# Attention and MLP kernel on one core: batch 0 in a listed order of steps, means from the division's sums, first q load and sum casts on ScalarE

## Chip, cores, metric

The kernel runs on one core of one Trainium2 chip. The metric is the device time of one launch in microseconds; lower is better. Most executions of one kernel lie within 1% of each other here, so a difference of a few tenths of a per cent needs several runs in the same rounds.

## The reference

Eight batches, eight heads, 576 tokens, head size 64. Causal attention with a bias from a running sum of `s`, then, token by token, an MLP whose output is added to its input:

```python
scores = scale * q @ k.T                       # per batch and head
cum    = cumsum(max(s, 0))
scores = where(causal, -1e9, scores + min(-(cum_i - cum_j), 0))
attn   = softmax(scores) @ v                   # [8, 8, 576, 64]
x      = attn.transpose(0, 2, 1, 3).reshape(8, 576, 512)
mu, var = mean(x), mean((x - mu)**2)           # per token
xn     = (x - mu) / sqrt(var + 1e-6) * g_ln
out    = x + max(xn @ w_ch1, 0) @ w_ch2        # 512 -> 2048 -> 512
```

## The kernel before

From batch 1 on, heads are interleaved with the MLP of the batch before, and TensorE is full. Batch 0 has no MLP before it to interleave with, so it runs in its own way, by token tiles: the rows of q, k and bias of 128 tokens are transposed, their scores, exponentials, value products, division and mean follow, and quarter "pieces" of the MLP's first product fill in. This stage (here "the front") ends where the heads of batch 1 begin. A "pair" is the q and k of two heads, w1 and w2 are the weights of the two products, loaded in four parts each, and rstd is the reciprocal deviation of the normalisation. The parts that matter below:

```python
def tile_pv(t, g):                     # value products, division, statistics of one tile
    ...
    nc.vector.reciprocal(out=rinv[:, 0:G], in_=pot[:, :, D])
    nc.vector.tensor_tensor(out=x..., in0=pot[:, :, 0:D], in1=rinv..., op=ALU.mult)
    nc.vector.bn_stats(out=st[0][:, t, g, :], in_=x)

def aug(gam, eng, h0=0):               # bias rows of a head group, four small copies in SBUF
    eng.dma_start(out=kq[i][D : D + 1, 1, h0:G, 0:S], in_=c_hi[r, :])
    for j in range(3):
        eng.dma_start(out=kq[i][D + 1 + j : D + 2 + j, 0, h0:G, 0:S], in_=c3[r, j, :])
...                                    # cut: the front's steps, in order
last_keys()                            # last scores of batch 0: the old bias rows are free
aug(2, nc.sync)                        # bias rows for the first heads of batch 1
piece(0, 3, "act")
tr_pair(4)                             # q and k of those heads, transposed
evac_pair("k", 4, ("dve", "dve"))
evac_pair("q", 4, ("act", "act"))
piece(1, 3, "dve")
last_pv(0)
last_pv(1)
bias_rows(trc)

for n in range(H, BH):                 # heads of batch 1 and later
    pre(n)                             # n == 8: loads of pairs 6, 7, w2(0), w2(1)
    ...                                # n == 10: loads of w2(2), w2(3), pair 8 (GpSimd's queue)
    scores(b, h)
    run_units(1, True)                 # hidden pieces of batch 0, then its output products
```

The softmax here doesn't subtract the row's maximum and nothing guards it: scores larger than these inputs give would overflow.

Of the kernel before, what the change touches and what calls it, by code (L numbers as in the profile page):

```python
# [15 lines left out]
P = 128  # L16
# [3 lines left out]
def kernel(  # L20
# [57 lines left out]
    mhalf = const.tile([P, 8], F32, name="mhalf")  # L78
    v_bf = [const.tile([P, NT, H, D + 1], BF16, name=f"v_bf{i}") for i in range(2)]
# [46 lines left out]
    def ld_tile(kind, t):  # L126
        tmp = stage.tile([P, H, D], F32, name="tiletmp", tag="st")
        nc.sync.dma_start(out=tmp, in_=tile_src(kind, t))
        loaded[kind, t] = tmp
# [123 lines left out]
    def cum_relu(c0, c1):  # L253
        nc.vector.tensor_scalar(
            out=c_in[:, c0:c1],
            in0=c_in[:, c0:c1],
            scalar1=0.0,
            scalar2=1.0 / scale,
            op0=ALU.max,
            op1=ALU.mult,  # L260
        )

    def cum_split(c0, c1):
        x, y, hi, mid, lo = (a[:, c0:c1] for a in (c_sc, c_in, c_hi, c_mid, c_lo))
        nc.vector.tensor_copy(out=hi, in_=x)
        nc.vector.tensor_tensor(out=y, in0=x, in1=hi, op=ALU.subtract)
        nc.vector.tensor_copy(out=mid, in_=y)
        nc.vector.tensor_tensor(out=lo, in0=y, in1=mid, op=ALU.subtract)
# [209 lines left out]
    def ln_xn(b, t):  # L478
        tiles = x_tiles(b)
        if t >= len(tiles):  # L480
            return
        ln_aggr(b, t)
        xn = xnp.tile([P, Dm], BF16, name="xn", tag="xn")
        nc.vector.scalar_tensor_tensor(  # L484
            out=xn,
            in0=tiles[t],
            scalar=mvs[b][:, t, 0:1],
            in1=gb,
            op0=ALU.subtract,
            op1=ALU.mult,  # L490
        )
        xns[b, t] = xn
        if t == len(tiles) - 1:
            ln_rstd(b)

    def ln_tr(b, t, eng="dve"):
# [3 lines left out]
        pool, tag = (ps_m, "m") if b == 0 else (ps_t, "tr")  # L500
        tr = pool.tile([P, KD, P], BF16, name="trx", tag=tag)
        for kd in range(KD):
            nc.tensor.transpose(tr[:, kd, :], xn[:, kd * P : (kd + 1) * P], ident)  # L503
        if t < NF:
# [91 lines left out]
    ld_tile("k", 0)  # L596
    ld_tile("q", 0)
# [40 lines left out]
    nc.gpsimd.memset(er[TL:P, :, OD : OD + TL], 0.0)  # L638
    nc.gpsimd.memset(er[:, :, OD + TL : EW], 0.0)
# [4 lines left out]
    ld_w1(3)  # L644

# [4 lines left out]
    trt = {}  # L650

    def tr_tile(t):
        pn = P if t < NF else TL
        for g in range(2):
            tr = ps_m.tile([P, 2, G, P], BF16, name="trt", tag="m")
            for u in range(2):
                for hh in range(G):
                    nc.tensor.transpose(  # L658
                        tr[0:KA, u, hh, 0:pn],
                        rowb[0:pn, t, u * H + g * G + hh, :],  # L660
                        ident[0:pn, 0:pn],
                    )
            trt[t, g] = tr

    def evac_tile(t, g, eng):
# [4 lines left out]
            trt.pop((t, g))[0:KA, :, :, 0:pn],  # L670
# [4 lines left out]
    def tile_bank(t, g, i):  # L675
        a = ps_s.tile([P, 512], F32, name="st", tag="s")
        for c in range(4):
            hh, kb = divmod(4 * i + c, t + 1)
            nc.tensor.matmul(
                a[:, c * P : (c + 1) * P],  # L680
                lhsT=kq[g][0:KA, 0, hh, kb * P : (kb + 1) * P],
                rhs=kq[g][0:KA, 1, hh, t * P : (t + 1) * P],
# [7 lines left out]
        o = (0, 2, 6, 0)[t] + g * (t + 1) + i  # L690
        nc.scalar.activation(out=er_slot(o), in_=a, func=ACT.Exp, scale=scale)
# [5 lines left out]

    def tile_pv(t, g):
        pot = ps_t.tile([P, G, D + 1], F32, name="pot0", tag="tr")
        for hh in range(G):  # L700
            for kb in range(t + 1):
                i, c = divmod(hh * (t + 1) + kb, 4)
                o = (0, 2, 6, 0)[t] + g * (t + 1) + i
                nc.tensor.matmul(
                    pot[:, hh, :],
                    lhsT=er_slot(o)[:, c * P : (c + 1) * P],
# [4 lines left out]
        rinv = small.tile([P, NT], F32, name="rinv", tag="rinv")  # L711
        nc.vector.reciprocal(out=rinv[:, 0:G], in_=pot[:, :, D])
        x = xb[0][:, t, g * 256 : (g + 1) * 256]
        nc.vector.tensor_tensor(
            out=x.rearrange("p (h d) -> p h d", d=D),
            in0=pot[:, :, 0:D],
            in1=rinv[:, 0:G].unsqueeze(2).to_broadcast([P, G, D]),
            op=ALU.mult,
        )
        nc.vector.bn_stats(out=st[0][:, t, g, :], in_=x)  # L720


    def last_bank(g, i):
        a = ps_s.tile([P, 512], F32, name="st", tag="s")
        for hh in range(G):
            for w in range(2):
                kb, c = 2 * i + w, (2 * hh + w) * TL
                nc.tensor.matmul(
                    a[:, c : c + TL],
                    lhsT=kq[g][0:KA, 0, hh, kb * P : (kb + 1) * P],  # L730
                    rhs=kq[g][0:KA, 1, hh, NF * P : S],
                    start=True,
                    stop=True,
                )
        nc.scalar.activation(out=er_slot(8 + 2 * g + i), in_=a, func=ACT.Exp, scale=scale)

    def last_keys():
        a = ps_s.tile([P, 512], F32, name="st", tag="s")
        for h in range(H):
            c = slice(h * TL, (h + 1) * TL)  # L740
            nc.tensor.matmul(
                a[0:TL, c],
                lhsT=kq[h // G][0:KA, 0, h % G, NF * P : S],
                rhs=kq[h // G][0:KA, 1, h % G, NF * P : S],
                start=True,
                stop=False,
            )
            nc.tensor.matmul(
                a[0:TL, c], lhsT=ident[:, 0:TL], rhs=maskT[:, 0:TL], start=False, stop=True
            )  # L750
        nc.scalar.activation(out=er_slot(0)[0:TL], in_=a[0:TL], func=ACT.Exp, scale=scale)

    def last_pv(g):
        pot = ps_t.tile([P, G, D + 1], F32, name="pot0", tag="tr")
        for hh in range(G):
            for kb in range(NT):
                h = g * G + hh
                if kb < NF:
                    c = (2 * hh + kb % 2) * TL
                    e = er_slot(8 + 2 * g + kb // 2)[:, c : c + TL]  # L760
                    vv = v_bf[0][:, kb, h, :]
                else:
                    e = er_slot(0)[0:TL, h * TL : (h + 1) * TL]
                    vv = v_bf[0][0:TL, kb, h, :]
                nc.tensor.matmul(
                    pot[0:TL, hh, :], lhsT=e, rhs=vv, start=(kb == 0), stop=(kb == NF)
                )
        rinv = small.tile([P, NT], F32, name="rinv", tag="rinv")
        nc.vector.reciprocal(out=rinv[0:TL, 0:G], in_=pot[0:TL, :, D])
        nc.vector.tensor_tensor(  # L770
            out=xm[0][0:TL, g * 256 : (g + 1) * 256].rearrange("p (h d) -> p h d", d=D),
            in0=pot[0:TL, :, 0:D],
            in1=rinv[0:TL, 0:G].unsqueeze(2).to_broadcast([TL, G, D]),
            op=ALU.mult,
        )


    def piece(c, t, eng):
        ph = ps_m.tile([P, 4, P], F32, name="ph", tag="m")
        cols = slice(t * P, (t + 1) * P)  # L780
        for j in range(4):
            fb = 4 * c + j
            for kd in range(KD):
                nc.tensor.matmul(  # L784
                    ph[:, j, :],
                    lhsT=w1_bf[:, kd, fb * P : (fb + 1) * P],
                    rhs=xTs[0][:, kd, cols],
                    start=(kd == 0),
                    stop=(kd == KD - 1),
                )  # L790
        dst = hT[:, 4 * c : 4 * c + 4, cols]
# [5 lines left out]
    def banks(t, g, *ii):  # L797
        for i in ii:
            tile_bank(t, g, i)

    R = (P, 2 * P, S)
    cum_relu(0, R[0])
    cum_scan(0, R[0])
    cum_split(0, R[0])
    cast_tile("k", 0, "act")
    cast_tile("q", 0, "act")
    cum_relu(R[0], S)
    bias_tr(0)
    bias_cols(0, 1)
    cum_scan(R[0], R[1])  # L810
    cum_split(R[0], R[1])
    keep_warm(1)
    tr_tile(0)
    evac_tile(0, 0, "act")
    bias_tr(1)
    evac_tile(0, 1, "dve")
    bias_cols(1, 2)
    cum_scan(R[1], S)
    keep_warm(2)
    banks(0, 0, 0)  # L820
    banks(0, 1, 0)
    tr_tile(1)
    evac_tile(1, 0, "act")
    evac_tile(1, 1, "dve")
    cum_split(R[1], S)
    tile_pv(0, 0)
    tile_pv(0, 1)
    banks(1, 0, 0, 1)
    for t in (2, 3, 4):
        bias_tr(t)  # L830
    bias_cols(2, NF)
    bias_cols(NF, NT, TL)
    banks(1, 1, 0, 1)
    tr_tile(2)
    evac_tile(2, 0, "act")
    evac_tile(2, 1, "dve")
    keep_warm(2)
    banks(2, 0, 0, 1, 2)
    tile_pv(1, 0)
    tile_pv(1, 1)  # L840
    ln_xn(0, 0)
    tr_tile(3)
    evac_tile(3, 0, "dve")
    evac_tile(3, 1, "dve")
    banks(2, 1, 0, 1, 2)
    ln_xn(0, 1)
    keep_warm(2)
# [169 lines left out]
```

## Time and profile before

| | before |
|---|---|
| time, first three runs | 378.47 us median (378.07 to 379.31) |
| profiled span | 376.9 us |
| TensorE busy, whole span | 96% |
| last matmul of batch 0's scores starts | 39.38 us |
| first scores of batch 1 start | 47.78 us |
| full TensorE clock again, for good | 53.58 us |

"L526" and the like are lines of the kernel's file; line numbers differ between versions, so read the operation and the tiles. "PE" is TensorE, "DVE" VectorE, "ACT" ScalarE, "POOL" GpSimd, "SPq" SyncE's issue of a DMA. The prediction shows the busy times by stretch, TensorE's waits and the chain of waits. Two more views of this kernel are needed later. GpSimd's timeline (start, length, what, and in brackets the idle time before it and what ended it):

```profile
35.78 1.05 POOL L473 TENSOR_TENSOR rstd<-rstd,mhalf 128x4 f32<-128x4 f32 x1 [8.00 <-DVE rstd L472]
...
40.13 2.29 POOL L212 DMA_DIRECT2D w_bf<-in_moe_w_ch_dram  x3
```

GpSimd stood 8.0 us for the input of batch 0's reciprocal deviations (rstd); the loads that stand behind it in the program were issued only then, the last three parts of w2 from 40.13 on (the last two at 40.9 and 41.6). VectorE's timeline, the first step on `s`:

```profile
3.67 0.22 DVE L254 TENSOR_SCALAR c_in<-c_in 64x128 f32<-64x128 f32 x1 [1.03 <-DMA c_in<-in_s_dram]
```

### The profile page before, as it was taken

What the parts mean: (1) busy time and instruction counts of PE and PEld (TensorE: products, weight loads), DVE (VectorE), ACT (ScalarE), POOL (GpSimd) and SP (SyncE); (2) the same over time, 40 slices, a digit from 0 to 9 for tenths busy, and PEclk for the clock granted to TensorE, in tenths of its full rate; (3) what the DMA queues carried; (4) which work ended last, traced back from release to release, by engine and by line L of the source; (5) the groups of instructions that cost most, each with busy time, mean ns of one, the idle gap of its engine ahead of it and who ended that gap; (6) DMA issues with size and microseconds to landing.
All of it is one profiled execution on the core that took longest, in us unless ns stands there. A gap on an engine that the chain in (4) does not pass through costs nothing.

```text
span 376.9 us, 8560 instructions
## 1 busy us (share of the span) xinstructions
PE 359.9 (96%) x3189; PEld 204.8 (54%) x3189; DVE 202.7 (54%) x532; ACT 187.0 (50%) x357; POOL 167.4 (44%) x447
## 2 busy tenths in 40 slices
PE   7888799998999999999999999999999999999995
PEld 2677645555555555555555555555555554444444
DVE  7676546879436753684357545844485573212211
ACT  3565459777773377327732773277327613411410
POOL 9872605758756457436466556365732201000000
PEclk9899969999999999999999999999999999999999
DMA  9999994599979699839897888598920011002013
GB/s 141 169 192 110 138 198 78 140 170 215 214 169 205 163 216 211 151 97 233 172 187 197 199 175 204 124 224 190 203 71 28 2 57 57 0 31 82 1 30 84
DMA packets 164266, 52.09 MB, mean 138 GB/s; under 512 B 152848, under 2 KB 159552, under 8 KB 164224
## 3 DMA queue, kind: packets, MB, share of 16 engines
q1 hardware_dynamic: 140432, 42.95, 51.3%
q0 software_dynamic: 23392, 8.06, 20.0%
q8 instruction: 25, 0.41, 0.5%
q10 hardware_dynamic: 400, 0.52, 0.4%
q14 instruction: 17, 0.14, 0.1%
HBM read 37.11 MB, written 9.44 MB: 124 GB/s over the span
## 4 chain that ended last, share of the span: by engine, by line
PE 82%; DVE 10%; DMA 3%; ACT 2%; issue 1%; SPq 1%; ACTq 0%; DVEq 0%
PE ph L516 31%; PE py L534 29%; PE pot L423 6%; DVE xn L484 3%; PE sc L347 3%; PE sa L347 3%; PE sb L347 3%; PE trx L503 2%; DMA kq<-c 1%; PE ph L784 1%; DMA tiletmp<-in_q_dram 1%; DVE stats L457 1%; PE trt L658 1%; DVE yo L543 1%; DVE kq L98 1%
## 5 line engine op out<-in xcount | busy, mean ns | idle before, releaser
L534 PE MATMUL py<-w_bf,hT 128*128 128x512 bf16 (+1 forms) x592 | 136.5, 373 | 0.5 <-DVE yo L543 0.5
L516 PE MATMUL ph<-xT,w_bf 128*128 128x512 bf16 x480 | 115.6, 383 | 0.0
L526 ACT ACTIVATE hT<-ph 128x512 bf16<-128x512 f32 x100 | 59.7, 597 | 65.2 <-PE ph L516 63.8
L534 PEld LDWEIGHTS <-hT 128*128 128x128 bf16 x592 | 53.5, 98 | 49.0 <-issue 1.0
L516 PEld LDWEIGHTS <-w_bf 128*128 128x128 bf16 x544 | 48.9, 98 | 51.0 <-issue 4.3
L366 POOL TENSOR_SCALAR_AFFINE_SELECT er<-er 128x128 bf16<-128x128 bf16 x216 | 59.2, 298 | 34.2 <-ACT er L358 34.0
L358 ACT ACTIVATE er<-sa 128x512 bf16<-128x512 f32 x56 | 33.4, 596 | 72.3 <-PE sa L347 43.1
L187 POOL CAST rows<-rowtmp 128x512 bf16<-128x512 f32 (+1 forms) x55 | 33.9, 617 | 53.2 <-DMA rowtmp<-in_q_dram 49.1
L524 DVE TENSOR_SCALAR hT<-ph 128x512 bf16<-128x512 f32 x36 | 24.9, 692 | 60.6 <-PE ph L516 59.8
L347 PEld LDWEIGHTS <-kq 68*128 68x128 bf16 x412 | 29.9, 98 | 24.3 <-issue 3.6
L423 PEld LDWEIGHTS <-er 128*128 128x128 bf16 x840 | 33.0, 98 | 13.3 <-issue 0.3
L543 DVE SCALAR_TENSOR_TENSOR yo<-py,rstd,xb 128x512 f32<-128x512 f32 x32 | 23.9, 748 | 25.9 <-PE py L534 21.2
L431 DVE RECIPROCAL rinv<-pot 128x5 f32<-128x5 f32 x56 | 10.8, 193 | 48.1 <-PE pot L423 47.9
L423 PE MATMUL pot<-v_bf,er 128*128 128x65 bf16 x840 | 34.7, 193 | 0.0
L358 ACT ACTIVATE er<-sc 128x512 bf16<-128x512 f32 x56 | 34.3, 613 | 0.0
L358 ACT ACTIVATE er<-sb 128x512 bf16<-128x512 f32 x56 | 33.6, 600 | 0.0
L473 POOL TENSOR_TENSOR rstd<-rstd,mhalf 128x4 f32<-128x4 f32 (+1 forms) x8 | 8.8, 1094 | 38.8 <-DVE rstd L472 38.8
L100 POOL CAST v_bf<-vtmp 128x512 bf16<-128x512 f32 (+1 forms) x30 | 18.8, 627 | 15.6 <-DMA vtmp<-in_v_dram 14.3
L484 DVE SCALAR_TENSOR_TENSOR xn<-xb,mv,gb 128x512 bf16<-128x512 f32 x32 | 24.3, 761 | 1.1
L433 DVE TENSOR_TENSOR xb<-pot,rinv 128x256 f32<-128x256 f32 x56 | 23.8, 424 | 1.9
L347 PE MATMUL sa<-kq 68*128 68x512 bf16 x56 | 21.6, 385 | 1.8 <-DMA kq<-c 1.8
L347 PE MATMUL sc<-kq 68*128 68x256 bf16 (+1 forms) x200 | 22.0, 227 | 0.2
(112 smaller groups left out, 372.2 us busy)
## 6 DMA issues: line engine op xcount, KB each, us to landing
out_dram<-yo SPq DMA_DIRECT2D x32, 256.0 KB
vtmp<-in_v_dram SPq DMA_DIRECT2D x24, 256.0 KB
rowtmp<-in_k_dram SPq DMA_DIRECT2D x44, 128.0 KB
rowtmp<-in_q_dram SPq DMA_DIRECT2D x44, 128.0 KB
w_bf<-in_moe_w_ch_dram POOLq DMA_DIRECT2D x8, 512.0 KB, 9.9
v_bf<-in_v_dram POOLq DMA_DIRECT2D x8, 128.0 KB, 7.9
kq<-rows SPq DMA_TRANSPOSE x55
kp<-in_k_dram POOLq DMA_DIRECT2D x6, 144.0 KB, 8.1
```

Of the source, the lines that this page charges most:

```text
L187: nc.gpsimd.tensor_copy(out=r[0:pn, :, :, 0:D], in_=loaded.pop(("rows", gam, t))[0:pn])
L347: nc.tensor.matmul(a[:, c + a0 - q0 : c + a1 - q0], lhsT=k_cols(b, h, kb), rhs=cols, start=True, stop=not (pe_mask and diag),)
L358: nc.scalar.activation(out=e[:, o : o + 512], in_=a, func=ACT.Exp, scale=scale)
L366: nc.gpsimd.affine_select(out=e[:, o : o + P], in_=e[:, o : o + P], compare_op=ALU.is_ge, fill=0.0, base=0, pattern=[[1, P]], channel_mult ...
L423: nc.tensor.matmul(pot[:, t, :], lhsT=e[:, o : o + P], rhs=vv[:, kb, h, :], start=(kb == 0), stop=(kb == last),)
L433: nc.vector.tensor_tensor(out=xb[b][:, :, hs], in0=pot[:, 0:NF, 0:D], in1=rinv[:, 0:NF].unsqueeze(2).to_broadcast([P, NF, D]), op=ALU.mult,)
L484: nc.vector.scalar_tensor_tensor(out=xn, in0=tiles[t], scalar=mvs[b][:, t, 0:1], in1=gb, op0=ALU.subtract, op1=ALU.mult,)
L516: nc.tensor.matmul(ph, lhsT=w1_bf[:, kd, fb * P : (fb + 1) * P], rhs=xT[:, kd, :], start=(kd == 0), stop=(kd == KD - 1),)
L524: nc.vector.tensor_scalar_max(out=hT[:, fb, :], in0=ph, scalar1=0.0)
L526: nc.scalar.activation(out=hT[:, fb, :], in_=ph, func=ACT.Relu)
L534: nc.tensor.matmul(py[0], lhsT=hT[:, fb, t * P : (t + 1) * P], rhs=w2_bf[:, fb, c0:c1], start=(fb == 0), stop=(fb == FB - 1),)
L543: nc.vector.scalar_tensor_tensor(out=yo, in0=py[0], scalar=rs, in1=x[:, c0:c1], op0=ALU.mult, op1=ALU.add)
```

## The change

The intent is a front with less idle time. All steps of batch 0 are cut small and put in one list, so that no engine waits for another's whole tile. VectorE, the fullest engine there, is relieved: the mean comes from the sum that the division gives along with its output, the statistics for the variance come later, and relu and casts of the running sum go to ScalarE. The first q load is issued from ScalarE. Loads of pairs 6, 7, w2(0) and w2(1) are queued earlier. The diff, cut to its core (lines left out are marked with dots):

```diff
-    ld_tile("k", 0)
-    ld_tile("q", 0)
+    ld_tile("k", 0, nc.sync)
+    ld_tile("q", 0, nc.scalar)
...
     ld_w1(3)
+    ld_cast_pair(6)
+    ld_w2(0)
+    ld_cast_pair(7)
+    ld_w2(1)
...                                   # in the division
-        nc.vector.tensor_tensor(..., op=ALU.mult)
-        nc.vector.bn_stats(out=st[0][:, t, g, :], in_=x)
+        nc.vector.scalar_tensor_tensor(
+            scalar=1.0, op0=ALU.mult, op1=ALU.mult, accum_out=sum0[:, t, g : g + 1], **args)
+    def tile_stats(t, g):
+        nc.vector.bn_stats(out=st[0][:, t, g, :], in_=xb[0][:, t, g * 256 : (g + 1) * 256])
...                                   # in the normalisation of batch 0
-        ln_aggr(b, t)
+        nc.vector.tensor_scalar(out=mean0[:, t : t + 1], in0=sum0[:, t, 0:1],
+            scalar1=sum0[:, t, 1:2], scalar2=1.0 / Dm, op0=ALU.add, op1=ALU.mult)
...                                   # the list; T transposes, e evacuation, S scores, x exp,
+    PLAN = """                       # V values, N division, B statistics, L mean and xn,
+        ...                           # X, y xT, M piece, r relu, P, pk, pq next pair, W zeros
+        M101 M102 x410 N30 M103 S411 Sk aug r10:A L3 P x411 B21 xk M020 M120 pk pq M121 M021
+        M022 M023 M122 M123 r02:D r12:A X3 S8 B11 y3:A M010 B00 M011 M130 B30 M012 M013 B10
+        M131 M132 r01:A M133 r13:A M110 M111 M112 M113 M030 M031 r11:A M032 M033 V40 r03:A
+        V41 N40 N41
+    """
...                                   # heads of batch 1: n == 8 has its scores in the list (S8)
-        if n == 8:
-            ld_cast_pair(6); ld_w2(0); ld_cast_pair(7); ld_w2(1)
-        scores(b, h)
+        if n > H:
+            scores(b, h)
...
+        if n == H + 1:
+            bias_rows(trc)
+            for t in range(NF):
+                ln_aggr(0, t)
+            ln_rstd(0)
```

`Sk` are the last scores of batch 0, `aug` the bias copies for the next heads, `S8` the first scores of batch 1.

## The prediction

> **What bounds the kernel now.** I read the page's head first, then the busy times by stretch, then TensorE's waits, then the chain of waits over the first 60 us, and last the timelines of TensorE, VectorE and ScalarE. The busy times by stretch (length, then busy us of PE, PEld, DVE, ACT and POOL, granted clock, DMA share, GB/s):
>
> ```profile
> 0.00:16.00 16.00, 11.55 (x107) 6.81 (x107) 11.93 (x42) 7.87 (x12) 14.28 (x24) 1.00 1.61 149
> 16.00:20.00 4.00, 3.97 (x38) 3.42 (x38) 0.90 (x4) 1.64 (x3) 3.04 (x8) 0.57 1.63 185
> 20.00:42.00 22.00, 18.74 (x368) 17.50 (x366) 15.48 (x37) 13.91 (x27) 12.60 (x17) 1.00 1.34 142
> 42.00:47.80 5.80, 3.16 (x41) 2.47 (x42) 3.59 (x8) 0.79 (x1) 1.69 (x3) 0.91 1.15 163
> 47.80:53.60 5.80, 5.80 (x28) 2.93 (x29) 1.41 (x4) 2.24 (x5) 0.00 (x0) 0.50 1.22 201
> ...
> 100.00:150.00 50.00, 50.00 (x439) 27.56 (x438) 26.91 (x77) 29.06 (x58) 27.54 (x85) 1.00 0.90 192
> ```
>
> From 100 us TensorE is full, and nothing there is edited. So the change is worth what it takes off the front, if nothing gives it back. In the front no engine is full: TensorE stalls, runs at half clock in 16 to 20 and in 47.8 to 53.6, and VectorE is busy 15.48 of 22 us in the middle. The end of the front, in the chain of waits (start, length, what):
>
> ```profile
> 39.38 0.77 SPq L221
> 40.20 0.60 SPq L223
> 40.84 1.15 SPq L223
> 42.03 5.62 DMA kq<-c
> 47.64 0.14 issue
> 47.78 0.58 PE sa L347
> ```
>
> The bias rows of the next head group (four copies, "aug") may be written only when the last scores of batch 0 have read the old ones. Their path is 39.4 to 47.65, 8.3 us: 2.65 us of issues ahead of the last one, then 5.62 to its landing. TensorE's own waits before and in that stretch:
>
> ```profile
> PE sa L347 <- DMA kq<-c: 1.8, 1, 1.8
> PE pot L765 <- ACT kq L96: 0.9, 1, 0.9
> ```
>
> Only 1.8 us is booked as waiting for that DMA, since TensorE still had 64 piece matmuls, 12 transposes and 40 value matmuls to do. The half clock behind it costs more: the four matmuls of 512 columns at 49.64 take 1.71 us, against 0.86 at 57.66. At 53.58, when the clock is full again, TensorE has done some 5.8/2 = 2.9 us of work since 47.78, of which 0.85 is the scores. In full-clock terms **the old front, with these scores, ends at 53.6 - 2.1 = 51.5 us**.
>
> **What the Trainium skill says.** (1) "TensorE: Matmul & The Clock Gate", Part 1: the array falls to half clock after an idle window of about 3.4 us, and the windows run free. The trace agrees in the size (1.71 against 0.86) and in granted clock 0.50; its half-clock stretches last 3.4 and 6.8 us. (2) "DMA: Bandwidth & Descriptors", Issuing engines are not separate DMA queues: another issuing engine saves only the time to start the transfer. Here one issue on SyncE is 0.57 to 0.59 us. (3) The same page, Queues, rings and completion order: each DMA engine takes packets from its queues in turn. So a q load in ScalarE's own row need not stand behind s and k in SyncE's; and a tiny copy still waits its turns beside a backlog, which 5.62 us for 4.5 KB agrees with. (4) "VectorE: DVE Perf Modes", Two Vector instructions with no wait between them: an operation that writes out its accumulator is two instructions. The kernel before has none, so its cost is open.
>
> **Part 1, q on ScalarE's queue, relu and casts on ScalarE.** Now q is issued at 2.08 and lands 5.20 later; its cast ends at 7.92 and the last 12 transposes of tile 0 start at 7.97. Earlier by 1.3 us of issue and out of the line, I expect it near 5.6. This isn't worth 1.5 us, because the plan puts both later scans (0.47 and 0.87) ahead of the first bias columns: the first split ends at 5.94, bias columns at 7.5, transposes 7.55 to 8.6, against 8.8 now. **Gain 0.2 us here**, but the splits of the later rows are then done early: lo of the last piece near 10.4 (now 13.8), so tile 1's and tile 2's transposes no longer wait for VectorE (0.4 and 0.9 us of TensorE waits).
>
> **Part 2, the listed order up to the last scores.** I walked the list by hand with the trace's durations: transposes of a tile's group 0.45, a score bank 0.3 to 0.45, exponentials 0.5 apart, evacuation on VectorE 0.62, on ScalarE 1.0, reciprocal 0.2, division 0.44, statistics 0.43, xn 0.75, a piece of 16 matmuls 0.9, relu on VectorE 0.62. VectorE is the fullest. From 5.94 to the evacuation ahead of the last bank: two scans 1.33, splits 1.5, bias columns 0.9, seven big evacuations 4.4, one small 0.36, eight divisions with reciprocal and an assumed 0.1 for the accumulator 5.9, three means with xn 2.85, three xT copies at 0.36, one relu 0.62, two statistics 0.8: **18.2 us**. Six of the eight statistics have left this stretch (2.6 us), the second relu of s (0.8) and two casts of the sums too. Their waits come out at about 1 us, so 25.3 us at best for that evacuation and 27.3 for the end of the last scores. TensorE has some 18.7 us of work up to there and ScalarE 17.5, so neither is the bound. Loads allow it, narrowly: the first and second parts of w1 were issued at 10.81 and 14.51 and took 9.4 and 9.8 us, so 20.2 and 24.3; the list wants them at about 20.4 and 25.6. A list walked by hand is never met: I add some 8%, 1.5 us, and take **28.8 us for the end of the last scores, against 39.4**. Part of that isn't gain: six of eight pieces now stand behind the last scores, against two before, so 64 matmuls, 3.6 us, have only moved.
>
> **Part 3, from there to the end of the front.** Behind the last scores the list has the 12 transposes, eight quarter pieces (1.8), the xT transposes, and then at once the next batch's first scores ("S8"). They need aug. TensorE reaches them at about 31.5 (the xT transposes wait for the pair's evacuation, 1.6 us). Aug costs 2.65 us of issues and 3 to 5.6 to landing; it lies beside a deeper backlog, because the loads of pairs 6 and 7 and two parts of w2 are now queued earlier, but in part beside small v packets. I take 4.5: 28.8 + 7.2 = 36.0. So **a stall of some 4.5 us** is in the new order, where 64 matmuls (3.6 us) and 40 value matmuls (1.3) stand behind the scores instead of in front. The clock will probably halve again: full loss of one window is 1.7 us, of two 2.9 with the overlap; I take 1.7. New end of the front: 36.0 + 0.85 scores + 3.6 + 1.3 + 1.7 = **43.4, against 51.5: 8.1 us saved**.
>
> **Part 4, what moves into the next stage.** Transposed bias rows to cT (0.94 + 0.70 + 0.37 + 0.28 with overlap, 2.0 us), four aggregates (0.2 each) and the rstd go behind the second head. VectorE is busy 3.03 of 6.4 us in 53.6 to 60, so they fit, but the next value matmuls share that buffer of PSUM: **0.3 us lost**. Sum 7.8; so 378.5 - 7.8 = 370.7, rounded for the upper tail of an earlier aug to **370.5**.
>
> **Rivals.** (a) *The aug wait replaces everything.* If aug takes the old 8.3 us and two half-clock windows follow, and the last scores end at 30.5, the front ends at 30.5 + 8.3 + 5.75 + 2.9 = 47.5: 4.0 saved, 374.5. For it: the backlog is deeper and the stall is longer than the old one. Against: half of the transfers there are smaller. (b) *Aug lands quickly, no half clock.* Last scores 28, landing after 5.6, then 5.75: 39.4, 12.1 saved, 366. For it: the list puts S8 early, which only makes sense where it doesn't wait. Against: the first packets of the old aug came over 4 us after issue. (c) *Loads become the bound.* The DMA engines are busy without a pause up to 37 us, and w2's last part lands at about 57. If TensorE comes 8 us earlier, the output projection wants that part at 60 instead of 68. It fits by 3 us; were it late, 2 to 3 us of the gain would go, 373. (d) *VectorE's accumulator is dear*, 0.3 instead of 0.1 us on eight divisions: 1.6 us lost, 372.
>
> **Range and chances.** (a) and (b) mark the ends: 366.0 to 374.5. The middle stands on the limit of 2% (370.9), so faster 0.53 and within 2% 0.45. A slowdown by 2% would need 7.6 us lost where the old front had the same waits: 0.02.
>
> **What would show it.** Right: the chain of waits has the last scores ending between 27.5 and 30.5, TensorE waiting 3 to 6 us for the bias copies ahead of the next scores, a granted clock of 0.5 for 3.4 or 6.8 us behind that, none in 16 to 20, and from 60 us on the same work some 8 us earlier. Part 1 is wrong if the first tile's transposes start before 7 us. Part 2 is wrong if TensorE waits long for loads of w1, q or v, or the last scores end after 32. Part 3 is wrong if the wait for the bias copies is under 2 us. Part 4 is wrong if TensorE's waits in 50 to 90 grow by over 1 us. What I'd have least foreseen is a later stage giving the gain back: that would show as equal starts after 100 us.

## The result, and the profile after

| | before | after |
|---|---|---|
| time, 4 runs each | 378.89 us median (378.07 to 380.81) | 375.04 us median (373.96 to 375.76) |
| ratio | 1 | 0.9889 (95%: 0.9841 to 0.9936) |
| profiled span | 376.9 us | 372.3 us |

A ratio is the mean time of one kernel's fast runs over that of the other's of the same rounds, so it isn't quite the ratio of the medians. All runs here are fast ones. The prediction was 370.5, with 366.0 to 374.5 as its range: the time lies just above it, and the gain is about half of what was forecast.

Busy times by stretch in the kernel after (length, busy us of PE, PEld, DVE, ACT, POOL, granted clock, DMA share, GB/s; the share can exceed 1 in this view):

```profile
20.00:27.20 7.20, 7.20 (x171) 6.94 (x168) 6.68 (x23) 6.07 (x12) 6.59 (x9) 1.00 1.32 199
27.20:30.10 2.90, 2.79 (x56) 2.63 (x52) 2.85 (x6) 2.86 (x6) 0.80 (x3) 1.00 2.32 162
30.10:36.00 5.90, 0.14 (x3) 0.00 (x0) 1.38 (x5) 0.33 (x1) 2.69 (x4) 0.73 1.83 177
36.00:43.10 7.10, 6.75 (x56) 5.98 (x57) 0.00 (x0) 3.40 (x6) 0.00 (x0) 0.50 1.22 195
43.10:45.50 2.40, 2.40 (x61) 2.29 (x60) 0.58 (x3) 1.19 (x2) 0.00 (x0) 1.00 0.49 79
45.50:54.00 8.50, 8.39 (x81) 4.84 (x80) 6.65 (x18) 6.64 (x13) 1.27 (x2) 1.00 0.01 3
```

Up to 30 us the list does what it was made for: TensorE is full, VectorE and ScalarE nearly so. Then comes a hole of 5.9 us with 0.14 us of work on TensorE, then 7.1 us at half clock (the trace's clock records have 0.5 from 32.83 to 43.07), and from 45.5 to 54 the DMA engines move 3 GB/s. The chain of waits through the hole:

```profile
29.31 6.60 DMA kq<-c
35.91 0.14 issue
36.04 0.58 PE sa L356
...
39.07 5.18 PE ph L805 x56
44.24 1.21 PE pot L761 x40
45.45 0.86 PE ph L536 x4
```

The last bias copy is issued at 29.31 and its landing releases the scores (`sa`) at 35.91. Behind them stand the piece matmuls (`ph L805`) and the value products (`pot`) that could have run in the hole. TensorE's waits, up to 42 us and from 60 to 150 us:

```profile
PE sa L356 <- DMA kq<-c: 5.8, 1, 5.8
...
PE py L554 <- DMA w_bf<-in_moe_w_ch_dram: 1.0, 1, 1.0
PE trqk L299 <- DMA qp<-in_q_dram: 0.4, 1, 0.4
```

The last two are new: the output product waits for a part of w2, and a transpose for a q load. GpSimd's timeline shows why:

```profile
52.73 1.05 POOL L482 TENSOR_TENSOR rstd<-rstd,mhalf 128x4 f32<-128x4 f32 x1 [18.14 <-DVE rstd L481]
53.75 1.55 POOL L214 DMA_DIRECT2D w_bf<-in_moe_w_ch_dram  x2
```

The rstd now waits for VectorE behind the second head of batch 1, GpSimd stands 18.1 us at it, and the last two parts of w2 are issued at 53.75 instead of 40.9. And VectorE's timeline at the start:

```profile
4.77 0.22 DVE L261 TENSOR_SCALAR c_in<-c_in 64x128 f32<-64x128 f32 x1 [2.14 <-DMA c_in<-in_s_dram]
```

`s` is there 1.1 us later than before. Where the gain stands, by the starts of the same work in TensorE's two timelines (a quarter is four matmuls of 512 columns):

| work | before | after | ahead by |
|---|---|---|---|
| last matmul of batch 0's scores | 39.38 | 27.25 | 12.1 |
| second head of batch 1, first scores | 53.83 | 47.65 | 6.2 |
| first output product, first quarter | 63.94 | 57.79 | 6.2 |
| the same, third quarter | 67.34 | 61.19 | 6.2 |
| second output product, first quarter | 70.69 | 66.22 | 4.5 |
| end of the span | 376.9 | 372.3 | 4.6 |

Half of the twelve microseconds goes in the hole and the half clock (some of it is moved work, as the prediction says), and another 1.7 at the late loads: the fourth quarter waits 0.98 us for w2 and starts at 63.20, and the wait for q follows it. The two timelines there, before and after:

```profile
67.34 1.89 PE L534 MATMUL py<-w_bf,hT 128*128 128x512 bf16 x8
```

```profile
61.19 1.03 PE L554 MATMUL py<-w_bf,hT 128*128 128x512 bf16 x4
63.20 1.02 PE L554 MATMUL py<-w_bf,hT 128*128 128x512 bf16 x4 [0.98 <-DMA w_bf<-in_moe_w_ch_dram]
```

### The profile page after: what moved, and what is told of

Read it like the earlier page. It is cut to its first block, busy times and chain, and to the rows that moved or that the text cites. A ratio compares the mean times of both kernels' runs of the same rounds, so it can differ in the third digit from the quotient of the medians.

```text
span 372.3 us, 8570 instructions
## 1 busy us (share of the span) xinstructions
PE 355.5 (95%) x3188; PEld 203.1 (55%) x3188; DVE 200.4 (54%) x540; ACT 187.7 (50%) x361; POOL 168.0 (45%) x446
## 4 chain that ended last, share of the span: by engine, by line
PE 75%; DMA 9%; DVE 5%; POOL 3%; SPq 2%; issue 2%; ACT 2%; POOLq 0%; ACTq 0%
PE py L554 27%; PE ph L536 27%; PE pot L432 5%; DMA qp<-in_q_dram 3%; PE sb L356 2%; PE sc L356 2%; PE sa L356 2%; DMA rowtmp<-in_q_dram 2%; DMA kq<-c 2%; DVE xn L503 2%; PE ph L805 2%; PE trx L521 2%; SPq L177 2%; PE st L703 1%; PE trt L681 1%
## 5 line engine op out<-in xcount | busy, mean ns | idle before, releaser
L536 PE MATMUL ph<-xT,w_bf 128*128 128x512 bf16 x480 | 113.8, 379 | 0.0
L432 PE MATMUL pot<-v_bf,er 128*128 128x65 bf16 x840 | 34.7, 193 | 0.0
L102 POOL CAST v_bf<-vtmp 128x512 bf16<-128x512 f32 (+1 forms) x30 | 18.3, 611 | 25.4 <-DMA vtmp<-in_v_dram 23.7
L503 DVE SCALAR_TENSOR_TENSOR xn<-xb,mv,gb 128x512 bf16<-128x512 f32 x28 | 21.8, 780 | 1.0
```

The lines of the kernel that those rows point to most:

```text
L432: nc.tensor.matmul(pot[:, t, :], lhsT=e[:, o : o + P], rhs=vv[:, kb, h, :], start=(kb == 0), stop=(kb == last),)
L503: nc.vector.scalar_tensor_tensor(out=xn, in0=tiles[t], scalar=mvs[b][:, t, 0:1] if b > 0 else mean0[:, t : t + 1], in1=gb, op0=ALU.subtrac ...
L536: nc.tensor.matmul(ph, lhsT=w1_bf[:, kd, fb * P : (fb + 1) * P], rhs=xT[:, kd, :], start=(kd == 0), stop=(kd == KD - 1),)
```

## Experiments

All kernels were checked for correctness on the chip and gave right results. "Ratio" is against the kernel before in the same rounds. Kernels of different calls (e1 to e4, e5 to e8, e9 to e12, e13 and e14) are compared by these ratios, which is less sharp than within one call.

| | edit to the changed kernel | median us | ratio (95%) |
|---|---|---|---|
| after | none | 375.04 | 0.9889 (0.9841 to 0.9936) |
| e1 | rstd later | 373.08 | 0.9848 (0.9810 to 0.9885) |
| e2 | S8 last | 367.72 | 0.9710 (0.9675 to 0.9744) |
| e3 | both | 365.71 | 0.9656 (0.9619 to 0.9693) |
| e4 | 24 zero matmuls in the wait | 374.77 | 0.9887 (0.9855 to 0.9920) |
| e5 | q on SyncE | 375.84 | 0.9905 (0.9831 to 0.9978) |
| e6 | e3 and q on SyncE | 364.73 | 0.9628 (0.9565 to 0.9691) |
| e7 | e1 and 24 zero matmuls | 373.12 | 0.9841 (0.9779 to 0.9903) |
| e8 | (kernel before) q on ScalarE | 381.44 | 1.0063 (0.9995 to 1.0132) |
| e9 | loads held back | 373.33, one run | |
| e10 | e11 with means from statistics | 365.92 | 0.9665 (0.9643 to 0.9686) |
| e11 | e6 and first values later | 364.76 | 0.9630 (0.9604 to 0.9656) |
| e12 | e11 with q on ScalarE | 366.19 | 0.9674 (0.9648 to 0.9700) |
| e13 | e1 and q on SyncE | 372.79 | 0.9808 (0.9775 to 0.9840) |
| e14 | e13 and 18 zero matmuls | 372.08 | 0.9781 (0.9745 to 0.9818) |

### e1: the rstd one head later

```diff
         if n == H + 1:
             ...
-            ln_rstd(0)
+        if n == H + 2:
+            ln_rstd(0)
```

> Edit: the rstd of batch 0 (a GpSimd power that waits for VectorE) is queued one head later, so that the loads of the last two parts of w2 and of pair 8 stand ahead of it on GpSimd's queue. Theory A (the loads were late because GpSimd stood 18.1 us waiting for the rstd's input at the head of its queue): those loads are issued near 35 us instead of 53.8, TensorE's waits for w_bf (1.0 us) and qp (0.4 us) disappear, and the time is 1.2 to 1.9 us below the changed kernel. Theory B (the DMA engines could not have brought them sooner): TensorE still waits about 1 us for w_bf and the time is within 0.4 us of the changed kernel.

GpSimd's timeline of e1:

```profile
33.84 1.61 POOL L214 DMA_DIRECT2D w_bf<-in_moe_w_ch_dram  x2 [0.43 <-DMA v_bf<-in_v_dram]
36.37 0.74 POOL L214 DMA_DIRECT2D w_bf<-in_moe_w_ch_dram  x1 [0.92 <-DMA w_bf<-in_moe_w_ch_dram]
```

The last two parts of w2 are issued at 34.7 (the second of the first line) and 36.4 and both waits of TensorE are gone. By the ratios the time falls by 0.41%, 1.6 us; the two intervals overlap, but e3 against e2, the same edit in the same rounds, gives 2.0 us. Theory A holds: the loads were late for their place behind a waiting instruction, not for want of DMA speed.

### e2 and e3: S8 behind its filler, and both edits

```diff
-        M022 M023 M122 M123 r02:D r12:A X3 S8 B11 y3:A M010 ...
+        M022 M023 M122 M123 r02:D r12:A X3 B11 y3:A M010 ...
-        V41 N40 N41
+        V41 S8 N40 N41
```

> Edit: the next batch's first scores (S8) are moved behind the pieces and value matmuls that stood behind them, nothing else. Theory A (the order puts TensorE in front of a copy that is not there, with 64 piece matmuls and 40 value matmuls as unused filler behind it, and the idle window halves the clock): the wait for the bias copies falls from 5.8 us to under 1.5 us, no or at most one half-clock window follows, the stage's end (first run of the next batch's first hidden piece) comes at 37 to 39 us instead of 45.3, and the time falls by 5.5 to 8 us, to 367 to 369.5. Theory B (the copies would simply be waited for elsewhere, or the front's end is set by the half clock from other causes): under 3 us gained.

> Edit: both of the above. If the two causes are separate: the sum of the two gains, some 7.5 to 9.5 us below the changed kernel, 365.5 to 367.5. If an earlier TensorE only meets late loads of w2 again: no better than the second edit alone by over 0.5 us.

The chain of waits of e2 at the place where the hole was:

```profile
34.24 1.95 PE ph L805 x32
36.19 1.21 PE pot L761 x40
37.40 0.30 PE sa L356
```

TensorE runs from the pieces through the values into the scores; no wait for the bias copies is left, and the granted clock is 1.00 from 29 us on. The ratio falls from 0.9889 to 0.9710, which is 6.8 us, for moving one word of the list. e3 is 8.8 us below the changed kernel by the ratios; the single gains sum to 8.3. So the two causes are separate, and theory A holds for both.

### e4 and e7: zero matmuls in the wait

```diff
-        ... X3 S8 B11 ...
+        ... X3 W9 W9 W6 S8 B11 ...     # e7: with e1's edit too
```

> Edit: 24 matmuls of zeros (about 5.2 us at full clock) in front of the scores that wait for the bias copies, so TensorE is busy in the wait; the wait itself stays. Theory A (the wait costs a second time by the halved clock, 7.1 us of work at half rate in 36.0 to 43.1, so 3.5 us): granted clock 1.0 behind the wait, time 2.5 to 4 us below the changed kernel. Theory B (the clock does not follow this idle time, or zeros don't count): clock 0.5 again and time unchanged within 0.7 us.

> Edit: rstd later (so that no load is late), and 24 matmuls of zeros in the wait for the bias copies. The zeros alone gave no time though the clock stayed full behind the wait; in that profile the loads held by the rstd took 2.4 us of TensorE's waits instead of 1.4. Theory A (the halved clock does cost a second time, and late loads ate the gain): 2 to 3.5 us below the rstd edit alone (373.1), so 369.6 to 371.1. Theory B (the half clock is not on the path, or the zeros cost what they save): within 0.7 us of it.

The clock stayed full behind the wait in both profiles, but neither kernel is faster than its base by more than 0.1%. This missed both forms of theory A; the time is as theory B of e7 has it, that the half clock is off the path or that the zeros cost what they save. In e7's profile the zeros run from 34.37 until the scores start at 39.98; from the last issue of the copies at 33.60 that is 6.4 us, so they may well have run past the landing (in e1 it was 4.9 us). The edit wasn't clean; e13 and e14 repeat it with fewer zeros.

### e5, e6, e8, e11, e12: which queue brings q

```diff
-    ld_tile("q", 0, nc.scalar)
+    ld_tile("q", 0, nc.sync)       # e5; e6: with the edits of e1 and e2 too
```

```diff
-    ld_tile("q", 0)                # e8: the kernel before
+    ld_tile("q", 0, nc.scalar)
```

```diff
-        S000 bc1 V01 x000 T10 N01 T11 tc2 e10:D e11:A V00 bc2 S100 N00 T20 ...
+        S000 bc1 x000 T10 T11 tc2 e10:D e11:A V01 V00 bc2 N01 S100 N00 T20 ...
                                    # e11: e6 and this; e12: e11 with nc.scalar for q
```

> Edit: the changed kernel with the first q load back on SyncE's queue behind s and k. Seen so far: with q on ScalarE's queue VectorE's first step on s starts at 4.77 to 5.25 us, against 3.67 in the kernel before; in three of the four edited kernels' profiles a half-clock window lay near 7.5 to 13.8 us and the last scores ended at 29 to 31 us instead of 27.4. Theory A (q in a row of its own takes turns with s and delays it, and the longer wait of TensorE at the start brings the early half-clock window): s is there at about 3.7 again, the first tile's transposes start near 8.0 us, and the time is 0.8 to 2.5 us below the changed kernel. Theory B (q, landing at 7.3 again, holds the first tile just as long): time within 0.6 us of the changed kernel.

> Edit: rstd later, first scores of the next batch last, q back on SyncE's queue. Theory A: 0.8 to 2.5 us below the version with the first two edits alone (365.7), so 363.2 to 365. Theory B: within 0.6 us of it.

> Edit: the kernel before with one part of the change alone, the first q load on ScalarE's queue. Theory A (it delays s by about 1.1 us; q comes some 1.4 us earlier, and the old order needs both at about the same time): s at 4.8 to 5.2, the first transposes 0.5 to 1 us later, time equal or up to 1 us worse than before. Prediction on record (worth a little): up to 1.5 us better.

> Edit: rstd later, first scores last, q on SyncE, and the value matmuls of tile 0 moved behind the transposes of tile 1 (with q on SyncE TensorE stood 1.15 us for v there). Expected if that wait is on the path: 0.7 to 1.2 us below the same kernel without the last edit (364.7), 363.3 to 364.2; if the loads hold the next tiles just as long, no change.

> Edit: the kernel e11 with the first q load on ScalarE's queue, as the change has it, in the same rounds. Theory A (s comes 1.1 us later, and the early half-clock window follows in some executions): 1 to 2.5 us slower than e11. Theory B (no matter): within 0.5 us.

In the changed order with the hole (e5) `s` came at 3.85 us again, but no difference in time can be told: 373.04 to 377.16 us. Theory A's gain of 0.8 to 2.5 us did not show there. Where the hole is gone it shows. e12 against e11, in the same rounds: 0.9674 against 0.9630, 1.7 us by the ratios, 1.4 by the medians. e6 against e3: 1.1 us, and e13 against e1, both with the hole: 1.5 us, in different rounds. The kernel before with q on ScalarE (e8) is 2.4 us slower by the ratio, with an interval that just includes none; I had expected at most 1. e11 itself brought nothing over e6: its wait for v was not on the path, and my expectation for it failed.

Why it costs, in TensorE's timelines of e11 and then of e12, the first tile's 16 transposes:

```profile
7.48 1.05 PE L681 MATMUL trt<-ident,rowb 128*68 128x128 bf16 x16 [0.31 <-DVE rowb L242]
```

```profile
9.23 1.89 PE L681 MATMUL trt<-ident,rowb 128*68 128x128 bf16 x16 [0.16 <-DVE rowb L242]
```

In e12 they start 1.75 us later and take 1.89 instead of 1.05 us: TensorE is at half clock. VectorE's first step on `s` is at 3.71 in e11 and 5.08 in e12. Over all profiles: with q on SyncE (before, e5, e6, e10, e11, e13, e14) that step starts at 3.66 to 3.89 and these transposes run at full clock in all seven. With q on ScalarE (after, e1 to e4, e7 to e9, e12) it starts at 4.77 to 5.25, and they ran at half clock, wholly or in part, in eight of nine profiles. The ninth is the changed kernel's own profile, at full clock: it shows the change at its best, and its run was the fastest of four. The last scores of the front then end at 29.2 to 31.7 us in the edited kernels with q on ScalarE, instead of 27.4. The timed runs agree: four of e12's five have a granted clock of 0.993 or 0.994 over the span, e11's four 0.998 or 1.0. A mean near 1 does not rule the early half clock out, though: in e1, e3, e7 and e9 the trace's clock records begin only after 13 us, and the half clock shows in the matmuls alone (16 transposes in 1.91 us; e3's mean is 0.999).

### e9: the backlog, taken away

```diff
     ld_w1(2)
-    for t in range(NT): ld_cast_v(1, t)
-    ld_w1(3); ld_cast_pair(6); ld_w2(0); ld_cast_pair(7); ld_w2(1)
...
+    nc.gpsimd.tensor_copy(out=mean0[:, 0:1], in_=er[:, 0, 0:1])   # waits for the exp of S8
+    for t in range(NT): ld_cast_v(1, t)
+    ld_w1(3); ld_cast_pair(6); ld_w2(0); ld_cast_pair(7); ld_w2(1)
```

> A look only; its time will be worse. Edit: the changed kernel with the loads of v of batch 1, the last part of w1, pairs 6 and 7 and two parts of w2 held on GpSimd's queue until the next batch's first exponential, so that the DMA engines are free when the bias copies are issued. Theory A (the copies are slow because they take turns with a backlog): from the last issue to the release of the scores 2 to 3 us instead of 6.6, TensorE's wait 1 to 2.5 us. Theory B (these 4.5 KB copies always take that long): 4.5 us or more, wait 4 us or more.

The chain of waits of e9:

```profile
32.76 1.70 DMA kq<-c
34.46 0.14 issue
34.59 0.38 PE sa L356
```

From the last issue to landing 1.70 us instead of 6.60; TensorE's wait is 0.9 us instead of 5.8. The DMA share was 0.02 from 32.7 to 34.5 us, against 1.90 from 29.3 to 36 in the kernel after. Theory A holds: the copies of 4.5 KB take that long because the DMA engines are busy with queued loads. I had expected a worse time; the one run (373.33) does not show it, though the held loads cost TensorE waits for w1 and w2 of 0.5, 0.5 and 2.4 us later.

### e10: means from the statistics again

```diff
-        nc.vector.scalar_tensor_tensor(..., accum_out=sum0[:, t, g : g + 1], **args)
+        nc.vector.tensor_tensor(op=ALU.mult, **args)
-    ... L0 ... L1 ... L2 ... L3 ...                  # and no statistics elsewhere
+    ... B00 B01 L0 ... B10 B11 L1 ... B20 B21 L2 ... B30 B31 L3 ...
```

> Edit: the kernel e11 with the means from the statistics again: plain division, both statistics and the aggregate ahead of each xn, no sums, no aggregates later. Theory A (VectorE is the fullest engine of the front, so six statistics of 0.35 us on the way to the last scores count): last scores 1 to 2.5 us later and the time 1 to 2 us above e11. Theory B (covered by other waits): within 0.5 us of e11.

0.9665 against 0.9630 of e11 in the same rounds: 1.3 us slower by the ratios (1.2 by the medians). The last scores end at 28.4 instead of 27.8, so 0.6 later where I expected 1 to 2.5; where the rest of the 1.3 us goes was not traced. This part of the change is worth what it was made for. VectorE's groups in the front of the kernel after (busy us, mean ns) show its price:

```profile
L786 DVE SCALAR_TENSOR_TENSOR xb<-pot,rinv 128x256 f32<-128x256 f32 x8 | 3.4, 425 | 0.3
L786 DVE DVE_READ_ACCUMULATOR xb<-pot,rinv 128x1 f32 x8 | 0.7, 83 | 0.0
```

The division takes 425 ns as before, and the read of the sum 83 ns, which in the timeline overlaps the next instruction.

### e13 and e14: the half clock by itself

```diff
+        ...                             # e13: the edits of e1 and e5, as above
-        ... X3 S8 B11 ...
+        ... X3 W9 W9 S8 B11 ...                      # e14: e13 and this
```

> Edit: the changed order with its wait for the bias copies, rstd later and q on SyncE, so that neither the late loads nor the early half-clock window blur the wait. Base for e14. Expected: wait of 4.5 to 5.5 us in front of the first scores, two half-clock windows behind it, time 372 to 374, and, against e11 in earlier rounds, 8 to 9 us for the wait and the clock together.

> Edit: e13 with 18 matmuls of zeros (3.9 us) in the wait, fewer than in e4 and e7, so that they end before the copies have landed. Theory A (the halved clock costs on its own): the clock stays 1.0 behind the wait, the stretch from the first scores to the next batch's first hidden piece falls from about 9 to about 7 us, and the time is 1.5 to 2.5 us below e13. Theory B (the half clock is covered by the waits for ScalarE there): within 0.7 us of e13.

TensorE's timeline of e13, from the released scores to the first hidden piece of batch 1's stage:

```profile
36.53 0.58 PE L356 MATMUL sa<-kq 68*128 68x512 bf16 x1 [5.21 <-DMA kq<-c]
...
39.56 5.09 PE L805 MATMUL ph<-xT,w_bf 128*128 128x128 bf16 x56 [0.31 <-ACT xT L98]
...
45.69 0.38 PE L536 MATMUL ph<-xT,w_bf 128*128 128x512 bf16 x1
```

and of e14:

```profile
35.89 0.38 PE L356 MATMUL sa<-kq 68*128 68x512 bf16 x1 [1.16 <-DMA kq<-c]
...
38.47 3.46 PE L805 MATMUL ph<-xT,w_bf 128*128 128x128 bf16 x56 [1.08 <-ACT xT L98]
...
42.98 1.03 PE L536 MATMUL ph<-xT,w_bf 128*128 128x512 bf16 x3
```

The stretch is 9.16 us at mostly half clock and 7.09 us at full clock: the half clock costs 2.1 us in the profiled executions. In the timed runs it is 1.0 us by the ratios (0.9808 and 0.9781), and the intervals overlap, so the size in the mean isn't settled (it lies between theory A's 1.5 to 2.5 us and theory B's 0.7); of six timed runs of e14, three still had a granted clock under 0.998 over the span. The rest of the hole is the wait itself: e13 differs from e6 only in the place of S8, and the ratios are 0.9808 and 0.9628, 6.8 us in different calls. Against e11 it is 6.7 us by the ratios, where I expected 8 to 9, and e13's half clock lasted 10.2 us, where I expected two windows (6.8).

## Why the prediction was half right

The mechanism was right: a faster front up to the last scores, a stall at the scores placed ahead of their data, a half clock behind it. The sum was 8.1 us of front minus 0.3, and the time fell by 3.9. In the profiles, 6.2 of the 8.1 us are there at the second head of batch 1 (1.9 short: part 3), and 1.7 go at the late loads where 0.3 was put (part 4); 4.6 are left at the end. The timed median gains less than this profile, whose run was the fastest of four and had no early half clock (part 1). By its steps:

- **Part 1 (q and relu on ScalarE, "gain 0.2 us")** failed. I wrote that q would be out of the line, and didn't ask what it takes from `s` when both share the same engines. `s` came 1.1 to 1.6 us later, and the half clock at the start followed in eight of nine profiles. The first transposes start at 8.36 us, where 7.55 was predicted; with q back on SyncE they start at 7.49 (e5), so it was the order of the scans that brought them forward. (The wait of 0.4 us that the text gives to the later tiles is tile 0's, at 6.91.) q on ScalarE costs 1.4 to 1.7 us in e12 against e11. That the delay brings the half clock on, rather than going along with it, is argued from the order of events.
- **Part 2 (last scores at 28.8)**: they end at 27.4 in the profile (the last matmul starts at 27.25), close to the bare walk of 27.3. The allowance for a walk never being met was not needed in that execution; with the early half clock of the other profiles it is too small. The terms listed for VectorE sum to 19.7, not 18.2: eight divisions are listed, but the order and the trace have six ahead of that evacuation, and with six the sum is 18.3. The means were worth 1.2 to 1.3 us (e10).
- **Part 3, the release**: 36.0 predicted, 36.04 measured, by two errors that cancel: scores 1.5 us earlier, copies slower (6.60 from the last issue, where I took 4.5 of a range of 3 to 5.6). The hint that small packets would ease the backlog was wrong; e9 shows that the backlog makes 4.9 of the 6.6 us. (What the text says of the old front's filler is misread as well: two pieces ran there, 32 matmuls at 39.51 and 40.92, not 64. No sum rests on it.)
- **Part 3, behind the release, is the larger mis-sized term**: 5.75 us of work plus 1.7 for the clock, so 43.4. Measured 45.45, 2.0 us more. At full clock (e14) the stretch takes 7.1 us instead of 5.75, mostly because the last xT evacuation stands behind three exponentials on ScalarE (1.08 us of wait), and the half clock adds 2.1.
- **Part 4 and rival (c)** failed. I put 0.3 us for moved VectorE work and said that w2 would come with 3 us to spare. I asked whether the DMA engines could bring it, and not whether GpSimd would issue it. Between the third quarter of the first output product and the second output product 1.7 us of the gain go; 1.6 us of time return in e1.
- **Rivals**: (a), at 374.5, came nearest. Its late last scores (30.5) are not in the changed kernel's own profile, but they are what the profiles with the early half clock show (29.2 to 31.7); the late loads are not in it. (b) did not occur. (d) did not occur: the accumulator's read costs 83 ns, hidden.

What each of the three places costs is thus shown by undoing it: 6.8 us lie in the place of S8, 1.6 in the place of the rstd, 1.4 to 1.7 in q's queue (measured where the hole is gone). My own sum missed only 4 of these, since 4.5 us of the stall and a part of the half clock stood in it. The best kernels here, e6 and e11, have the change without these three: 364.7 us, 3.7% below the kernel before.

## What to carry to other kernels

In a queue that keeps its order, ask of every waiting instruction what stands behind it that could run: on TensorE one set of scores ahead of its data cost 6.8 us with enough work right behind it, and on GpSimd one small power function held two large loads for 18 us. A tiny copy beside a backlog is not quick (here 6.6 us instead of 1.7), so count its landing from the backlog, not from its size. A load that is moved to another queue to come sooner may delay the loads beside it, as q did `s` by 1.1 to 1.6 us; move it only if those can wait.

## What the Trainium skill lacked or had wrong

- "TensorE: Matmul & The Clock Gate", Part 1, gives about 3.4 us of sustained work to come back to full clock, but not how much idle time they may hold. Here the half-clock stretches lasted 3.4, 6.8 and 10.2 us. After the hole TensorE was busy 3.1 of the 3.4 us from 36.24 to 39.66, with one wait of 0.31 us, and the clock stayed at half; it was full after the next 3.4 us, which had no gap. e5 and e13 show the same.
- "DMA: Bandwidth & Descriptors", Anatomy of one DMA, has a fixed cost of about 2 us, fitted for DMAs of GpSimd (these copies are SyncE's), and no figure for a small copy beside a backlog of GpSimd's loads. Here 4.5 KB took 1.70 us from issue to landing with free engines (e9) and 6.60 beside the backlog.
- No page says what a read of VectorE's accumulator costs: 83 ns in the profile, without a visible delay of the next instruction.
